# A GELU feed-forward block: the opening loads issued from two engines, b1 from a third, and the warm-up fed from a constant

## The chip, the cores and the metric

The kernel runs on one NeuronCore of a Trainium2 chip. The metric is the device time of one execution in microseconds (us); lower is better. Before the change the median of 3 runs is 96.36 us (96.36 to 96.37).

## The reference

The reference is a two-layer feed-forward block in bfloat16 for 2048 tokens, 448 features and 1792 hidden units:

```python
def reference(x, w1, b1, w2, b2):          # x (1,2048,448), w1 (448,1792), w2 (1792,448)
    h = jnp.einsum("bsd,df->bsf", x, w1) + b1
    h = jax.nn.gelu(h, approximate=True)
    return jnp.einsum("bsf,fd->bsd", h, w2) + b2
```

## The kernel before

**Layers and chunks.** The 2048 tokens are cut into four chunks of 512 columns. Layer 1 ("l1") of a chunk computes 14 tiles of 128 hidden units by 512 tokens. The 448 features are contracted in three full 128-row slices and a remainder of 64 rows; two tiles of neighbouring hidden units run their remainders at the same time on the two halves of TensorE's rows (`half`, line 226), and the full slices run as passes of 512 columns (`full`, line 218). ScalarE applies GELU with the bias `b1_f` to each finished tile (line 326). Layer 2 ("l2", line 303) multiplies the result with w2, and VectorE adds b2 (line 345). TensorE's order is written out by hand: l1 of chunks 0 and 1, l2 of chunk 0, l1 of chunk 2, l2 of chunk 1, and so on. Eight PSUM banks are used in turn.

**The opening.** Layer 1 needs x with features on the partitions. For chunks 1 to 3 the DMA transposes x on the way in (line 154). For chunk 0, x is loaded plainly in two halves into `xn_sb` (lines 162 and 163), TensorE transposes it with sixteen small matmuls against an identity (line 203), and VectorE and ScalarE copy the six results from PSUM to `xT_sb` (lines 339 and 322). b1 is loaded as 14 rows of 128 and turned by one more small matmul (line 194), which stands between the second and the third group of transposes. Before all that TensorE runs eleven passes of 256 columns over a tile of zeros (line 189), whose results are never used.

**The first block of layer 1** (`opening_block`) takes eight tiles of hidden units side by side, one to a PSUM bank: eight passes with the first feature slice (k = 0), eight with the second (k = 1), then the third slices and the remainders: 24 full passes, and 8 halves, which run in pairs. The waits in it are on pieces of w1: k = 0 in two column pieces (`sem_w10[0]` and `sem_w10[1]`, line 136), k = 1, 2 and 3 for the first 1024 hidden units (`sem_w1[k]`, line 140), and, ahead of the next block, the "rest", which is the other 768 hidden units in two transfers (`sem_w1r`, lines 141 and 144). The eighth pass of k = 0 goes to the bank that the turned b1 occupied, so it waits for VectorE's copy of b1 (`sem_b1`).

**The queues.** SP issues, in this order: x's two halves, w1 k = 0 in two pieces, w1 k = 1, 2, 3, the rest of w1 in two transfers, four transposing loads of x's chunk 1, w2 in two parts, b2, the other eight transposing loads, and then the output. ScalarE issues only the b1 load at the start and one output at the end. GpSimd builds the identity and issues nothing.

Of the kernel before, what the change touches and what calls it, by code (L numbers as in the profile page):

```python
# [5 lines left out]
ACT = mybir.ActivationFunctionType  # L6
ALU = mybir.AluOpType
BF16 = mybir.dt.bfloat16
FP32 = mybir.dt.float32


def bass_standalone__dense_activation_gelu__prompt_kernel(
# [8 lines left out]
    B, S, D = x.shape  # L21
    F = w1.shape[1]
    P = 128
# [8 lines left out]
    NFT = F // P  # L32

    KROW = [0, 128, 256, 320]
    NKT = len(KROW)

    WCUT = 8 * P

    W0_PIECES = [(0, 4), (4, 8)]
# [12 lines left out]
    XBANK = 1  # L52
    NB = 8

    NWARM = 11
    WN = 256

    OCUT = 256
# [21 lines left out]
    with ExitStack() as es:  # L80
# [3 lines left out]
        w2_sb = sb("wo_sb", [P, NFT, D], BF16)  # L84
        xn_sb = sb("xn_sb", [P, STC, D], BF16)
        ident = sb("ident", [P, P], BF16)
        zeros = sb("zeros", [P, WN], BF16)
        act_junk = sb("act_junk", [P, 8], BF16)
        b1n_sb = sb("bin_sb", [NFT, P], BF16)
        b1_f = sb("bi_f", [P, NFT], FP32)  # L90
# [8 lines left out]
        sem_w1r = S_("sem_w1r")  # L99
# [2 lines left out]
        sem_xn = [S_(f"sem_xn{i}") for i in range(2)]  # L102
        sem_b1n = S_("sem_b1n")
        sem_x = [None] + [S_(f"sem_x{i}") for i in range(1, NSC)]
        sem_zero = S_("sem_zero")
        sem_id = S_("sem_id")
        sem_xtp = S_("sem_xtp")
        sem_xTd = S_("sem_xTd")
# [21 lines left out]
            src = ps[XBANK + n][:, 0:2 * P * len(parts)]  # L130
            return to, src.rearrange("p (k t) -> p k t", k=len(parts))

        def load_w1(eng):
            with nc.allow_non_contiguous_dma(reason="w1 column pieces"):
                for i, (a, b) in enumerate(W0_PIECES):
                    eng.dma_start(  # L136
                        w1_sb[:, 0, a * P:b * P], w1[0:P, a * P:b * P]
                    ).then_inc(sem_w10[i], 16)
                for k, r in list(enumerate(KROW))[1:]:
                    eng.dma_start(w1_sb[:, k, 0:WCUT], w1[r:r + P, 0:WCUT]).then_inc(sem_w1[k], 16)  # L140
                eng.dma_start(  # L141
                    w1_sb[:, 0:3, WCUT:F], w1[0:3 * P, WCUT:F].rearrange("(k p) f -> p k f", p=P)
                ).then_inc(sem_w1r, 16)
                eng.dma_start(w1_sb[:, 3, WCUT:F], w1[KROW[3]:D, WCUT:F]).then_inc(sem_w1r, 16)

        def load_w2(eng, i):
            a, b = W2_PIECES[i]
# [12 lines left out]
        @block.sync  # L160
        def _(sp):
            sp.dma_start(xn_sb[:, 0:2, :], x0_view[:, 0:2, :]).then_inc(sem_xn[0], 16)  # L162
            sp.dma_start(xn_sb[:, 2:4, :], x0_view[:, 2:4, :]).then_inc(sem_xn[1], 16)  # L163
            load_w1(sp)
            load_xT(sp, 1)
            for i in range(len(W2_PIECES)):
                load_w2(sp, i)
            sp.dma_start(b2_bc[:, :], b2.partition_broadcast(P)).then_inc(sem_b2, 16)
            for c in range(2, NSC):
                load_xT(sp, c)  # L170
            for j in range(NST - 1):
                sp.wait_ge(sem_osb, j + 1)
                sp.dma_start(out_dram(j), out_sb[:, j, :]).then_inc(sem_od, 16)
            sp.wait_ge(sem_od, 16 * NST)

        @block.gpsimd
        def _(pool):
            pool.memset(ident[:, :], 0.0).then_inc(sem_id, 1)  # L178
            pool.wait_ge(sem_id, 1)
            pool.affine_select(  # L180
                out=ident[:, :], in_=ident[:, :], compare_op=ALU.not_equal, fill=1.0,
                base=0, pattern=[[-1, P]], channel_multiplier=1,
            ).then_inc(sem_id, 1)

        @block.tensor
        def _(pe):
            pe.wait_ge(sem_zero, 1)
            for _i in range(NWARM):
                pe.matmul(ps[0][:, 0:WN], lhsT=zeros[:, 0:P], rhs=zeros[:, :], start=True, stop=True)  # L189
            pe.wait_ge(sem_id, 2)  # L190
            for n, (_, parts) in enumerate(XPARTS):
                if n == 2:
                    pe.wait_ge(sem_b1n, 16)
                    pe.matmul(  # L194
                        ps[NB - 1][:, 0:NFT], lhsT=b1n_sb[:, :], rhs=ident[0:NFT, 0:NFT],
                        start=True, stop=True,
                    ).then_inc(sem_b1T, 1)
                for h, k in parts:
                    if (h, k) in ((0, 0), (1, 0)):
                        pe.wait_ge(sem_xn[h], 16)  # L200
                    for t in range(2):
                        col = parts.index((h, k)) * 2 * P + t * P
                        mm = pe.matmul(  # L203
                            ps[XBANK + n][:, col:col + P],
                            lhsT=xn_sb[:, 2 * h + t, KROW[k]:KROW[k] + P],
                            rhs=ident[:, :],
                            start=True, stop=True,
                        )
                mm.then_inc(sem_xtp, 1)
# [7 lines left out]
            def full(c, ft, k, start, stop):  # L217
                return pe.matmul(  # L218
                    bank("g", order.index((c, ft)))[:, :],
                    lhsT=w1_sb[:, k, ft * P:(ft + 1) * P],  # L220
                    rhs=xT_sb[:, k, c * SC:(c + 1) * SC],
                    start=start, stop=stop,
                )
# [11 lines left out]

            def opening_block(first, second):

                fts = first + second
                for n, ft in enumerate(fts):
                    for i, (a, _) in enumerate(W0_PIECES):  # L240
                        if ft == a:
                            pe.wait_ge(sem_w10[i], 16)
                    if n == 0:
                        pe.wait_ge(sem_xTd, 2)
                    elif n == NB - 1:
                        pe.wait_ge(sem_b1, 1)
                    elif XPARTS[n - XBANK][0] == "a":
                        pe.wait_ge(sem_xTa, sum(e == "a" for e, _ in XPARTS[:n - XBANK + 1]))
                    elif n - XBANK >= 4:
                        pe.wait_ge(sem_xTd, sum(e == "d" for e, _ in XPARTS[:n - XBANK + 1]))  # L250
                    full(0, ft, 0, True, False)
                pe.wait_ge(sem_w1[1], 16)
                for n, ft in enumerate(fts):
                    full(0, ft, 1, False, False)
                pe.wait_ge(sem_w1[2], 16)
                pe.wait_ge(sem_w1[3], 16)
                for n, ft in enumerate(first):
                    full(0, ft, SLOTS[n % 2][2], False, False)
                for n, ft in enumerate(first):
                    half(0, ft, *HALVES[n % 2], False, True).then_inc(sem_l1, 1)  # L260
                for n, ft in enumerate(second):
                    half(0, ft, *HALVES[n % 2], False, False)
                for n, ft in enumerate(second):
                    full(0, ft, SLOTS[n % 2][2], False, True).then_inc(sem_l1, 1)
# [48 lines left out]

        @block.scalar
        def _(act):
            act.dma_start(b1n_sb[:, :], b1.rearrange("(c p) -> c p", p=P)).then_inc(sem_b1n, 16)
            act.wait_ge(sem_zero, 1)
            act.activation(act_junk[:, :], zeros[:, 0:8], ACT.Gelu_apprx_tanh)  # L318
            for n, (e, parts) in enumerate(XPARTS):
                if e == "a":  # L320
                    act.wait_ge(sem_xtp, n + 1)
                    act.copy(*x_part(n, parts)).then_inc(sem_xTa, 1)  # L322
            act.wait_ge(sem_b1, 1)
            for i, (c, ft) in enumerate(order):
                act.wait_ge(sem_l1, i + 1)
                act.activation(  # L326
                    g_sb[:, ft, c * SC:(c + 1) * SC], bank("g", i)[:, :], ACT.Gelu_apprx_tanh,
                    bias=b1_f[:, ft:ft + 1], scale=1.0,
                ).then_inc(sem_g, 1)
            act.wait_ge(sem_osb, len(outs))  # L330
            act.dma_start(out_dram(NST - 1), out_sb[:, NST - 1, :]).then_inc(sem_od, 16)

        @block.vector
        def _(dve):
            dve.memset(zeros[:, :], 0.0).then_inc(sem_zero, 1)  # L335
            for n, (e, parts) in enumerate(XPARTS):
                if e == "d":
                    dve.wait_ge(sem_xtp, n + 1)
                    dve.tensor_copy(*x_part(n, parts)).then_inc(sem_xTd, 1)  # L339
            dve.wait_ge(sem_b1T, 1)  # L340
            dve.tensor_copy(b1_f[:, :], ps[NB - 1][:, 0:NFT]).then_inc(sem_b1, 1)  # L341
            dve.wait_ge(sem_b2, 16)
            for n, (j, c0, c1) in enumerate(outs):
                dve.wait_ge(sem_l2, n + 1)
                dve.tensor_tensor(  # L345
                    out=out_sb[:, j, c0:c1], in0=bank("o", n)[:, 0:c1 - c0], in1=b2_bc[:, c0:c1],
                    op=ALU.add,
                ).then_inc(sem_osb, 1)
# [28 lines left out]
```

## Time and profile before

| what | value |
|---|---|
| median of 3 runs | 96.36 us (96.36 to 96.37) |
| the profiled execution, own time | 96.84 us |
| its span, first to last instruction | 95.1 us |
| TensorE (PE) busy | 90.5 us, 95% of the span |
| ScalarE (ACT) busy | 36.1 us, 38% |
| VectorE (DVE) busy | 11.9 us, 13% |
| x halves to `xn_sb`, issue to landing | 2.6 and 2.7 us |
| w1 k = 0 pieces, issue to landing | 3.6 and 3.7 us |
| w1 k = 1 to 3, issue to landing | 4.3 to 5.1 us |
| w1 rest, issue to landing | 7.4 and 7.6 us |

The profiled execution lasted 0.48 us longer than the median of the plain runs, and 1.74 us of its own time lies outside the span. A line of the timeline gives start, length, engine, source line, operation, tiles (written <- read) and count; in brackets stands how long the engine had been idle and what ended the idleness. "SPq" and "ACTq" are an engine's instruction queue, where DMAs are issued; "PEld" is the weight load of a matmul. Matmuls are pipelined, so the length of one is more than the distance from one start to the next.

### The profile page before, as it was taken

The numbers are of one execution on the slowest core, as the hardware profiler recorded it, in microseconds if no ns is written. First come the engines' busy times: TensorE is split into PE (matmuls) and PEld (weight loads), VectorE is DVE, ScalarE is ACT, GpSimd is POOL, SyncE is SP. The second block draws the span as 40 slices with busy tenths as digits, with TensorE's granted clock in tenths as the row PEclk, the third lists the DMA queues.
The fourth block names the chain that finished last, engine by engine and source line by source line (L and its number), as shares of the span: only waits on it lengthen the run. The fifth ranks groups of instructions, "written<-read, shape, count | busy, mean of one in ns | idle before, by whom it ended". The sixth has DMA issues, their size and how long they took to land.

```text
span 95.1 us, 1155 instructions
## 1 busy us (share of the span) xinstructions
PE 90.5 (95%) x484; PEld 43.8 (46%) x490; DVE 11.9 (13%) x22; ACT 36.1 (38%) x61; POOL 0.7 (1%) x6
## 2 busy tenths in 40 slices
PE   5999989999999999999999999999999999999990
PEld 4654243434345555434335555434435555555670
DVE  0240000000000222200000222200000222222130
ACT  3340699959495000049586000039577000000000
POOL 2000000000000000000000000000000000000000
DMA  1899999996520111010000111010000110111111
GB/s 37 257 310 320 101 210 340 358 146 118 108 55 0 48 48 48 22 33 0 0 3 0 48 48 35 13 55 0 0 0 0 48 40 14 43 48 55 48 48 48
DMA packets 12385, 7.50 MB, mean 79 GB/s; under 512 B 7004, under 2 KB 11996, under 8 KB 12380
## 3 DMA queue, kind: packets, MB, share of 16 engines
q1 hardware_dynamic: 12208, 7.31, 32.1%
q10 hardware_dynamic: 172, 0.12, 0.4%
q8 instruction: 4, 0.07, 0.2%
q14 instruction: 1, 0.01, 0.0%
HBM read 4.02 MB, written 1.84 MB: 62 GB/s over the span
## 4 chain that ended last, share of the span: by engine, by line
PE 84%; DMA 8%; SPq 4%; issue 1%; DVE 0%
PE ps L303 45%; PE ps L218 33%; DMA wi_sb<-in_w_dram 8%; PE ps L226 6%; SPq L140 1%; SPq L136 1%; SPq L141 0%; SPq L163 0%; SPq L162 0%; DVE out_sb L345 0%
## 5 line engine op out<-in xcount | busy, mean ns | idle before, releaser
L326 ACT ACTIVATE g_sb<-ps,bi_f 128x512 bf16<-128x512 f32 x56 | 33.3, 700 | 33.8 <-PE ps L226 33.8
L303 PE MATMUL ps<-wo_sb,g_sb 128*128 128x448 bf16 (+2 forms) x238 | 42.9, 341 | 0.0
L218 PE MATMUL ps<-xT_sb,wi_sb 128*128 128x512 bf16 x162 | 37.2, 379 | 1.0 <-issue 0.5
L303 PEld LDWEIGHTS ps<-wo_sb,g_sb 128*128 128x128 bf16 x238 | 23.1, 98 | 19.7
L218 PEld LDWEIGHTS ps<-xT_sb,wi_sb 128*128 128x128 bf16 x168 | 15.6, 98 | 21.8 <-issue 3.6
L345 DVE TENSOR_TENSOR out_sb<-ps,bo_bc 128x448 bf16<-128x448 f32 (+2 forms) x17 | 10.2, 597 | 76.8 <-PE ps L303 76.8
L226 PE MATMUL ps<-xT_sb,wi_sb 64*128 64x512 bf16 x56 | 7.4, 379 | 0.0
L226 PEld LDWEIGHTS ps<-xT_sb,wi_sb 64*128 64x128 bf16 x56 | 2.1, 94 | 4.8 <-issue 3.4
L189 PE MATMUL ps<-zeros 128*128 128x256 bf16 x11 | 2.5, 418 | 1.1 <-DVE zeros L335 1.1
L189 PEld LDWEIGHTS ps<-zeros 128*128 128x128 bf16 x11 | 1.5, 143 | 1.6 <-DVE zeros L335 1.1
L322 ACT CAST xT_sb<-ps 128x256 bf16<-128x256 f32 (+1 forms) x3 | 1.3, 443 | 1.8 <-PE ps L203 1.8
L339 DVE CAST xT_sb<-ps 128x256 bf16<-128x256 f32 (+1 forms) x3 | 1.5, 514 | 3.4 <-PE ps L203 3.4
L203 PE MATMUL ps<-ident,xn_sb 128*128 128x128 bf16 x16 | 1.8, 287 | 0.0
L318 ACT ACT_TABLE_LOAD x1 | 1.3, 1283 | 1.4 <-PEq L362 1.4
L203 PEld LDWEIGHTS ps<-ident,xn_sb 128*128 128x128 bf16 x16 | 1.4, 132 | 0.4 <-issue 0.4
L180 POOL TENSOR_SCALAR_AFFINE_SELECT ident<-ident 128x128 bf16<-128x128 bf16 x1 | 0.3, 294 | 0.2 <-POOL ident L178 0.2
L335 DVE MEMSET zeros<- 128x128 uint32 x1 | 0.2, 165 | 0.8 <-PEq L362 0.8
L318 ACT ACTIVATE act_junk<-zeros 128x8 bf16<-128x8 bf16 x1 | 0.2, 208 | 0.0
L178 POOL MEMSET ident<- 128x128 bf16 x1 | 0.2, 205 | 0.3 <-POOLq L362 0.3
L194 PE MATMUL ps<-ident,bin_sb 14*128 14x14 bf16 x1 | 0.2, 188 | 0.0
L194 PEld LDWEIGHTS ps<-ident,bin_sb 14*128 14x128 bf16 x1 | 0.1, 97 | 0.2 <-issue 0.2
L341 DVE COPY bi_f<-ps 128x14 f32<-128x14 f32 x1 | 0.2, 163 | 0.0
(4 smaller groups left out, 0.4 us busy)
## 6 DMA issues: line engine op xcount, KB each, us to landing
out_dram<-out_sb SPq DMA_DIRECT2D x15, 112.0 KB, 1.7
wo_sb<-in_w_dram SPq DMA_DIRECT2D x2, 784.0 KB, 6.6
wi_sb<-in_w_dram SPq DMA_DIRECT2D x3, 256.0 KB, 4.7
wi_sb<-in_w_dram SPq DMA_DIRECT2D x1, 576.0 KB, 7.4
xn_sb<-in_x_dram SPq DMA_DIRECT2D x2, 224.0 KB, 2.7
wi_sb<-in_w_dram SPq DMA_DIRECT2D x2, 128.0 KB, 3.7
wi_sb<-in_w_dram SPq DMA_DIRECT2D x1, 192.0 KB, 7.6
xT_sb<-in_x_dram SPq DMA_TRANSPOSE x12, 4.0
```

The lines of the kernel that those rows point to most:

```text
L136: eng.dma_start(w1_sb[:, 0, a * P:b * P], w1[0:P, a * P:b * P]).then_inc(sem_w10[i], 16)
L140: eng.dma_start(w1_sb[:, k, 0:WCUT], w1[r:r + P, 0:WCUT]).then_inc(sem_w1[k], 16)
L189: pe.matmul(ps[0][:, 0:WN], lhsT=zeros[:, 0:P], rhs=zeros[:, :], start=True, stop=True)
L203: mm = pe.matmul(ps[XBANK + n][:, col:col + P], lhsT=xn_sb[:, 2 * h + t, KROW[k]:KROW[k] + P], rhs=ident[:, :], start=True, stop=True,)
L218: return pe.matmul(bank("g", order.index((c, ft)))[:, :], lhsT=w1_sb[:, k, ft * P:(ft + 1) * P], rhs=xT_sb[:, k, c * SC:(c + 1) * SC], sta ...
L226: return pe.matmul(bank("g", order.index((c, ft)))[:, :], lhsT=w1_sb[lo:lo + HALF, k, ft * P:(ft + 1) * P], rhs=xT_sb[lo:lo + HALF, k, c * ...
L303: mm = pe.matmul(bank("o", n)[:, 0:c1 - c0], lhsT=g_sb[:, ft, j * P:(j + 1) * P], rhs=w2_sb[:, ft, c0:c1], start=(ft == 0), stop=(ft == NF ...
L318: act.activation(act_junk[:, :], zeros[:, 0:8], ACT.Gelu_apprx_tanh)
L322: act.copy(*x_part(n, parts)).then_inc(sem_xTa, 1)
L326: act.activation(g_sb[:, ft, c * SC:(c + 1) * SC], bank("g", i)[:, :], ACT.Gelu_apprx_tanh, bias=b1_f[:, ft:ft + 1], scale=1.0,).then_inc( ...
L339: dve.tensor_copy(*x_part(n, parts)).then_inc(sem_xTd, 1)
L345: dve.tensor_tensor(out=out_sb[:, j, c0:c1], in0=bank("o", n)[:, 0:c1 - c0], in1=b2_bc[:, c0:c1], op=ALU.add,).then_inc(sem_osb, 1)
```

## The change

The change touches only the first microseconds of the program.

- x's second half, w1's second k = 0 piece and w1's k = 2 slice are issued by ScalarE; SP keeps x's first half, the first k = 0 piece, k = 1, k = 3 and the rest.
- b1 is loaded by GpSimd, after it has built the identity.
- The matmul that turns b1 moves from the transposes into the opening block, behind seven of the eight k = 0 passes. The eighth k = 0 pass moves to just ahead of the eighth k = 1 pass.
- The tile of zeros, its memset on VectorE and `sem_zero` are gone. The warm-up passes read the built-in constant 1.0 and wait for nothing of VectorE, and there are 13 of them instead of 11. ScalarE's first activation reads a built-in 0.0.

```diff
-    NWARM = 11
+    NWARM = 13
...
-        def load_w1(eng):
+        def load_w1(eng, which):
...
         def _(sp):
             sp.dma_start(xn_sb[:, 0:2, :], x0_view[:, 0:2, :]).then_inc(sem_xn[0], 16)
-            sp.dma_start(xn_sb[:, 2:4, :], x0_view[:, 2:4, :]).then_inc(sem_xn[1], 16)
-            load_w1(sp)
+            load_w1(sp, [("0", 0), 1, 3, "rest"])
             load_xT(sp, 1)
...
             ).then_inc(sem_id, 1)
+            pool.dma_start(b1n_sb[:, :], b1.rearrange("(c p) -> c p", p=P)).then_inc(sem_b1n, 16)
 
         @block.tensor
         def _(pe):
-            pe.wait_ge(sem_zero, 1)
+            ones_w = nc.const_aps.tensor(1.0, [P, P], BF16)
+            ones_x = nc.const_aps.tensor(1.0, [P, WN], BF16)
             for _i in range(NWARM):
-                pe.matmul(ps[0][:, 0:WN], lhsT=zeros[:, 0:P], rhs=zeros[:, :], start=True, stop=True)
+                pe.matmul(ps[0][:, 0:WN], lhsT=ones_w, rhs=ones_x, start=True, stop=True)
             pe.wait_ge(sem_id, 2)
             for n, (_, parts) in enumerate(XPARTS):
-                if n == 2:
-                    pe.wait_ge(sem_b1n, 16)
-                    pe.matmul(
-                        ps[NB - 1][:, 0:NFT], lhsT=b1n_sb[:, :], rhs=ident[0:NFT, 0:NFT],
-                        start=True, stop=True,
-                    ).then_inc(sem_b1T, 1)
...
                 fts = first + second
-                for n, ft in enumerate(fts):
+                for n, ft in enumerate(fts[:-1]):
...
-                    elif n == NB - 1:
-                        pe.wait_ge(sem_b1, 1)
...
                     full(0, ft, 0, True, False)
+                pe.wait_ge(sem_b1n, 16)
+                pe.matmul(
+                    ps[NB - 1][:, 0:NFT], lhsT=b1n_sb[:, :], rhs=ident[0:NFT, 0:NFT],
+                    start=True, stop=True,
+                ).then_inc(sem_b1T, 1)
                 pe.wait_ge(sem_w1[1], 16)
                 for n, ft in enumerate(fts):
+                    if n == NB - 1:
+                        pe.wait_ge(sem_b1, 1)
+                        full(0, ft, 0, True, False)
                     full(0, ft, 1, False, False)
...
         def _(act):
-            act.dma_start(b1n_sb[:, :], b1.rearrange("(c p) -> c p", p=P)).then_inc(sem_b1n, 16)
-            act.wait_ge(sem_zero, 1)
-            act.activation(act_junk[:, :], zeros[:, 0:8], ACT.Gelu_apprx_tanh)
+            act.dma_start(xn_sb[:, 2:4, :], x0_view[:, 2:4, :]).then_inc(sem_xn[1], 16)
+            load_w1(act, [("0", 1), 2])
+            zero = nc.const_aps.tensor(0.0, [P, 8], FP32)
+            act.activation(act_junk[:, :], zero, ACT.Gelu_apprx_tanh)
...
-            dve.memset(zeros[:, :], 0.0).then_inc(sem_zero, 1)
```

`load_w1` takes a list of the parts to issue on the given engine: `("0", i)` is piece i of k = 0, a number is that k, and `"rest"` stands for the two last transfers. The transfers themselves have the same shapes as before.

## The prediction

> **What bounds the kernel now.** The summary says that PE is busy for 95% of the span, so I read the chain that ended last, in order of time, to find where it leaves PE.
>
> ```profile
> 4.02 0.43 SPq L141
> 4.45 0.04 issue
> 4.50 7.63 DMA wi_sb<-in_w_dram
> 12.12 0.05 issue
> 12.17 2.76 PE ps L218 x12
> ```
>
> From 12.17 to the end the chain is PE, without a gap above 0.16 us. Before 12.17 it is SP's row of issues and the landing of the last w1 rest at 12.12. So the change, all of it ahead of 12.17, is worth what it moves the start of the second block, and nothing else. What PE itself did up to there is in the timeline of the opening.
>
> ```profile
> 0.83 0.17 DVE L335 MEMSET zeros<- 128x128 uint32 x1 [0.83 <-PEq L362]
> ...
> 1.05 2.53 PE L189 MATMUL ps<-zeros 128*128 128x256 bf16 x11 [1.05 <-DVE zeros L335]
> ...
> 3.50 0.58 PE L203 MATMUL ps<-ident,xn_sb 128*128 128x128 bf16 x4
> ...
> 4.02 0.19 PE L194 MATMUL ps<-ident,bin_sb 14*128 14x14 bf16 x1
> ...
> 4.14 1.25 PE L203 MATMUL ps<-ident,xn_sb 128*128 128x128 bf16 x12
> ...
> 5.45 3.14 PEld L218 LDWEIGHTS ps<-xT_sb,wi_sb 128*128 128x128 bf16 x16 [0.23 <-DMA wi_sb<-in_w_dram]
> ```
>
> The transposes begin as x's first half lands (issue 0.74 plus 2.6). The opening block begins at 5.45, 0.23 us after PE could have, on w1's first k = 0 piece (issue 1.66 plus 3.6 or 3.7). In a narrow window its last full pass starts at 11.50, and passes start 0.216 us apart, so the opening block is done at 11.72 and PE loses 0.45 us to the rest of w1. There are thus two DMA gates, 0.23 and 0.45 us, around a PE chain. Then I asked in half microseconds how well the DMA engines were fed.
>
> ```profile
> 2.00:2.50 0.50, 0.50 (x4) 0.33 (x3) 0.00 (x0) 0.50 (x1) 0.00 (x0) 1.00 0.63 182
> ...
> 3.00:3.50 0.50, 0.50 (x3) 0.13 (x2) 0.00 (x0) 0.00 (x0) 0.00 (x0) 1.00 0.97 354
> 3.50:4.00 0.50, 0.50 (x5) 0.32 (x4) 0.09 (x1) 0.00 (x0) 0.00 (x0) 1.00 0.91 196
> 4.00:4.50 0.50, 0.50 (x6) 0.46 (x6) 0.34 (x1) 0.37 (x1) 0.00 (x0) 1.00 0.51 139
> 4.50:5.00 0.50, 0.50 (x8) 0.50 (x6) 0.42 (x1) 0.21 (x1) 0.00 (x0) 1.00 0.70 199
> ```
>
> The last two columns are the DMA engines' busy share and GB/s. They move 354 at 3.0, but 139 to 199 from 3.5 to 5.0, just when w1's 128 KB pieces are due, of which SP issues one every 0.46 us. After 5.0 the share is 0.9 and over.
>
> **The change part by part**, on the profiled execution's clock.
>
> Warm-up: PE need not wait for VectorE's memset. GpSimd and SP begin their own work at 0.73 and 0.74, so PE starts at 0.75, 0.30 us earlier. Eleven passes started 0.211 us apart (1.05 to 3.16), so thirteen end at 0.75 + 13 x 0.211 = 3.50, against 3.37 before.
>
> x: the halves are issued at 0.74 side by side instead of at 0.74 and 1.20, and share the engines. The first half can't land before 3.35; it hardly lands after 3.9, when both had landed before. I take 3.55, nearer to the early end, since the share of 0.63 at 2.0 leaves room for a second feeder. The transposes then start at 3.65 instead of 3.50.
>
> Transposes: b1's matmul leaves. Four transposes from 3.50 would have let the fifth start at 3.88; it started at 4.14, so 0.26 us goes, and the second half, then landed, puts no wait in its place. Early transposes start 0.107 us apart, the last ones 0.055 (5.12 and 5.17 in narrow windows): PE's real pace doubles at about 5.0, 3.95 us after its first warm-up pass, though the clock column says 1.00 all along. With PE starting 0.30 us earlier, the pace rises between 4.7 and 5.0; I take 4.9. Twelve transposes from 3.65 at 0.107 reach 4.93, four at 0.055 reach 5.15. PE was through them at 5.23 before, so PE itself gains only 0.08 us here.
>
> The Trainium skill ("TensorE: Matmul & The Clock Gate", section "Part 1: The HAM clock gate (the "warmup" mystery)") says that the clock rises after a busy window of about 3.4 us which runs freely and doesn't start with the kernel. By that rule the earlier start buys no fixed 0.30 us, and the rise may stay at 5.0: 0.05 us or so of my sum.
>
> w1's first k = 0 piece: issued at 1.20 instead of 1.66. With the same 3.7 us it lands at 4.9; with ScalarE's 128 KB piece moving beside it at 325 GB/s (the row of 6 to 9 us), 0.4 later, 5.3. The opening block starts at 5.2, range 5.05 to 5.4, instead of 5.45.
>
> Opening block: it took 6.27 us (5.45 to 11.72). b1's matmul now stands in it, 0.12 us by the distance 4.02 to 4.14. The passes are the same ones. It ends at 5.2 + 6.39 = 11.59. The new wait of PE for b1 has 17 full passes and all halves queued behind it. GpSimd's load isn't in the trace: it is issued at about 1.5 (the identity's last step runs from 1.17 to 1.46) and is needed at 5.2 + 7 x 0.216 = 6.7. The landing times in the trace run from 1.7 to 7.6 us; at 2.7, the row nearest in time and load, b1 is there at 4.2, at the far end at 9.1. I take nothing. The second wait, for VectorE's copy (0.16 us), has seven passes of cover, 1.5 us.
>
> w1's rest: issued 1.45 us earlier (SP has three issues fewer ahead of it). If the landing kept its 7.6 us it would come at 10.7; if bytes alone decide, it stays at 12.1. The idle shares from 1.5 to 5.0 add up to 0.96 us of all engines; half of it won back gives 11.65. I take that.
>
> The Trainium skill ("DMA: Bandwidth & Descriptors", section "Issuing engines are not separate DMA queues") speaks against the change: DMAs of all issuers run on the same 16 engines, and a second issuer saves only issuing time, which is usually small. The row of 4.00 to 4.50, share 0.51, shows engines that were waiting for something; by the rule alone the gate would stay near 12.1.
>
> The rest: ScalarE's three issues cost 0.41 to 0.65 us each (rows of SP's L163 and of its own L316), so its table load (1.28) and first activation (0.21) end at 3.6 to 4.3 instead of 2.9; its first copy, at 4.12 before, moves to at most 4.35 and is needed by the third pass, at 5.6. Without that cover of 0.9 us PE would wait the difference. SP's transposing loads, w2 and b2 move up by at most 1.45 us; w2 is needed at 28.1, so nothing is gained, and the transposing loads still queue behind the rest of w1.
>
> Sum: the second block starts at 11.70 (the gate at 11.65, then the same 0.05), 0.47 us earlier. The profiled execution goes from 96.84 to 96.37, and the median by the same amount, from 96.36 to 95.89. The median was 0.48 below the profiled time, and I can't tell whether the 0.45 us gate is part of that; it stays in the range.
>
> **The rivals.**
>
> No change, a transfer or a PE chain that doesn't move: either the rest of w1 lands at 12.1 again, because the slowest engine's bytes decide (for it: 0.9 and over busy from 5 to 9 us), or plain runs have no DMA gate and PE's own chain decides, where 0.08 gained and 0.12 lost cancel. It gives 96.2 to 96.5. Against it: two gates would have to vanish together, or the starved stretch be of no use. Chance 0.20.
>
> Slower, PE's pace: both halves of x land only at 3.9, PE is idle from 3.50 to 4.0, and the rise of its pace is counted anew, 3.95 us from 4.0, to 7.95. The sixteen slow transposes last to 5.71. An opening pass at the slow pace costs 0.422 (twice 0.211), so 5.3 of 28 slots are done by 7.95, and the other 22.7 x 0.216, 0.22 of gaps and 0.12 for b1 bring the block's end to 13.19, the second block to 13.24: 1.07 later, 97.4. It decides from the point where the rise comes after about 6.1, since each us of delay costs half a us and the block has 12.12 - 11.59 = 0.53 to spare. For it: sharing x is sure, and the warm-up ends 0.15 ahead of my start of the transposes. Against it: a gap of half a us is short beside 2.8 us of work before it. Chance 0.15; b1 landing after 9.1 (98.2) or the like, 0.05.
>
> **How the numbers follow.** Faster has 0.60: 0.47 gained, own range 95.45 (opening from 5.05, rest in time, pace up at 4.7) to 96.15 (the first gate alone gains). A measurement of this kernel can tell about 0.2%, or 0.19 us, from no change. The range goes from 95.45 through no change to 96.9, a rise of the pace at about 7.1; it leaves out the worse half of the slower cases and a little below, under 0.2 together.
>
> **What would show it.** Right: warm-up passes from 0.75; x's halves landing within 0.2 us of each other at 3.4 to 3.7; no b1 matmul among the transposes; opening passes from about 5.2; DMA shares above 0.8 from 3.5 to 5.0; the second block from about 11.7. Wrong: the rest of w1 still ending PE's idleness at 12.1; opening passes starting over 0.4 us apart; PE idle in front of the b1 matmul.

## The result, and the profile after

The change made the kernel slower: a median of 97.31 us over 22 executions against 96.50 us for the kernel before over 22 beside it, a ratio of 1.006 (95% interval 1.0041 to 1.0079). On two other occasions the changed kernel, unedited or as good as unedited, came to 1.0034 (1.0013 to 1.0055) and 1.0042 (1.0017 to 1.0067). The three executions of the kernel before that were shown first, 96.36 to 96.37, lay near the low end of its 96.22 to 97.20. A few executions of most kernels here are some 2 us longer than the rest; the ratios leave these out, the medians hold them.

The profiled execution after the change lasted 97.52 us, its span 95.7. The chain that ended last (start, length, what):

```profile
1.66 6.42 DMA wi_sb<-in_w_dram
8.08 0.05 issue
8.13 2.98 PE ps L221 x13
11.11 0.97 PE ps L229 x8
12.08 3.56 PE ps L221 x16
```

The transfer in the chain is no longer the rest of w1, but k = 1, issued at 1.66 and landed at 8.08. Before, k = 1 had landed at 6.93 and nobody waited for it. From 8.13 on PE runs through; the second block has lost its gate. The timeline of the opening shows the rest:

```profile
0.79 2.93 PE L198 MATMUL ps<-const-bfloat16-1.0 128*128 128x256 bf16 x13 [0.79 <-PEq L372]
...
4.09 1.69 PE L206 MATMUL ps<-ident,xn_sb 128*128 128x128 bf16 x16 [0.37 <-DMA xn_sb<-in_x_dram]
...
5.61 1.67 PE L221 MATMUL ps<-xT_sb,wi_sb 128*128 128x512 bf16 x7
...
7.22 0.09 PEld L255 LDWEIGHTS ps<-ident,bin_sb 14*128 14x128 bf16 x1 [0.42 <-DMA bin_sb<-in_b_dram]
...
8.13 2.98 PE L221 MATMUL ps<-xT_sb,wi_sb 128*128 128x512 bf16 x13 [0.73 <-DMA wi_sb<-in_w_dram]
```

In the kernel before, the first twenty opening passes had run through without a gap:

```profile
5.45 4.49 PE L218 MATMUL ps<-xT_sb,wi_sb 128*128 128x512 bf16 x20
```

After the change, PE starts to warm up 0.26 us earlier and then waits for x; the transposes start at 4.09, not 3.50; the opening passes at 5.61, not 5.45; the b1 matmul follows them at 7.22, just after b1's landing at 7.17; and in front of the k = 1 passes PE stands idle for 0.8 us. The opening block ends at 12.89. Before, the second block had started at 12.17, so it starts 0.72 us later; the first pass of layer 2 shows nearly the same difference, 28.63 against 27.93. The page's list of DMA issues (issuer, KB each, median us to landing) has the reason, two lines from before and four from after:

```profile
wi_sb<-in_w_dram SPq DMA_DIRECT2D x3, 256.0 KB, 4.7
xn_sb<-in_x_dram SPq DMA_DIRECT2D x2, 224.0 KB, 2.7
...
wi_sb<-in_w_dram SPq DMA_DIRECT2D x2, 256.0 KB, 6.5
wi_sb<-in_w_dram ACTq DMA_DIRECT2D x1, 256.0 KB, 6.6
xn_sb<-in_x_dram SPq DMA_DIRECT2D x1, 224.0 KB, 3.2
xn_sb<-in_x_dram ACTq DMA_DIRECT2D x1, 224.0 KB, 3.4
```

A 256 KB slice took a median of 4.7 us to land before and 6.5 or 6.6 now, half of x 2.7 and now 3.2 or 3.4. What was issued side by side landed side by side: x's halves at 3.95 and 4.13 (3.37 and 3.90 before), k = 1 and k = 2 at 8.08 and 8.31 (6.93 and 7.77 before). And in half microseconds, the last columns being the DMA engines' share and GB/s:

```profile
4.00:4.50 0.50, 0.41 (x5) 0.44 (x6) 0.00 (x1) 0.00 (x0) 0.00 (x0) 1.00 0.94 195
4.50:5.00 0.50, 0.50 (x8) 0.50 (x6) 0.50 (x2) 0.29 (x1) 0.00 (x0) 1.00 0.98 201
```

The stretch that I had read as starved engines is still slow, 195 and 201 GB/s, with the engines now busy 0.94 and 0.98 of the time. The second issuer filled the idle shares, and no more bytes moved for it.

### The profile page after: what moved, and what is told of

Same layout as the page of the kernel before. It is cut to its first block, busy times and chain, and to the rows that moved or that the text cites. A ratio compares the mean times of both kernels' runs of the same rounds, so it can differ in the third digit from the quotient of the medians.

```text
span 95.7 us, 1164 instructions
## 1 busy us (share of the span) xinstructions
PE 91.3 (95%) x492; PEld 44.2 (46%) x492; DVE 11.9 (12%) x21; ACT 35.9 (38%) x61; POOL 1.3 (1%) x7
## 4 chain that ended last, share of the span: by engine, by line
PE 89%; DMA 7%; SPq 1%; DVE 0%; issue 0%
PE ps L313 44%; PE ps L221 37%; PE ps L229 7%; DMA wi_sb<-in_w_dram 7%; SPq L145 0%; SPq L170 0%; DVE out_sb L355 0%
## 5 line engine op out<-in xcount | busy, mean ns | idle before, releaser
L221 PE MATMUL ps<-xT_sb,wi_sb 128*128 128x512 bf16 x168 | 38.3, 380 | 0.7 <-DMA wi_sb<-in_w_dram 0.7
L198 PE MATMUL ps<-const-bfloat16-1.0 128*128 128x256 bf16 x13 | 2.9, 414 | 0.8 <-PEq L372 0.8
L198 PEld LDWEIGHTS ps<-const-bfloat16-1.0 128*128 128x128 bf16 x13 | 1.8, 141 | 1.5 <-issue 0.8
L191 POOL DMA_DIRECT2D bin_sb<-in_b_dram x1 | 0.6, 647 | 0.2 <-issue 0.2
```

Source lines behind the costliest of these rows:

```text
L191: pool.dma_start(b1n_sb[:, :], b1.rearrange("(c p) -> c p", p=P)).then_inc(sem_b1n, 16)
L198: pe.matmul(ps[0][:, 0:WN], lhsT=ones_w, rhs=ones_x, start=True, stop=True)
L221: return pe.matmul(bank("g", order.index((c, ft)))[:, :], lhsT=w1_sb[:, k, ft * P:(ft + 1) * P], rhs=xT_sb[:, k, c * SC:(c + 1) * SC], sta ...
```

## The experiments

Three theories were to be told apart. O, order: two issuers' transfers share the DMA engines, so what is needed first lands together with what is needed later. G: GpSimd's load of b1 is the cost. C: the warm-up, or idleness in it, moves the rise of PE's pace. All ratios are to the kernel before, run beside the experiment; the diffs are abridged to the calls that move.

**k = 2 back on SP.**

```diff
-load_w1(sp, [("0", 0), 1, 3, "rest"]);  load_w1(act, [("0", 1), 2])
+load_w1(sp, [("0", 0), 1, 2, 3, "rest"]);  load_w1(act, [("0", 1)])
```

> The changed kernel with one edit: w1's k = 2 slice goes back to SP, behind k = 1. Theory O (two issuers share the DMA engines, so what is needed first lands together with what is needed later): k = 1 no longer shares with k = 2, lands at 6.9 to 7.4 instead of 8.08, PE's idle stretch in front of the k = 1 passes falls from 0.8 us to 0.2 or less, and the time goes back to the kernel before within 0.2% (ratio 0.998 to 1.002). Theory G (GpSimd's load of b1 is what holds, by landing at 7.17 and by disturbing the others): b1 still lands at about 7.2 and the ratio stays at 1.004 to 1.008. Theory C (the earlier and longer warm-up moves the rise of PE's pace): nothing changes, 1.006.

Measured: 0.9998 (0.9973 to 1.0023). With this one edit no loss is left that could be told. PE's timeline:

```profile
4.23 1.09 PE L206 MATMUL ps<-ident,xn_sb 128*128 128x128 bf16 x16 [0.51 <-DMA xn_sb<-in_x_dram]
5.48 1.67 PE L221 MATMUL ps<-xT_sb,wi_sb 128*128 128x512 bf16 x7 [0.16 <-DVE xT_sb L349]
7.09 0.18 PE L255 MATMUL ps<-ident,bin_sb 14*128 14x14 bf16 x1
7.20 2.76 PE L221 MATMUL ps<-xT_sb,wi_sb 128*128 128x512 bf16 x12
```

k = 1 landed at 5.73, earlier than expected, b1 at 5.91, and the passes run through. x's first half is as late as in the changed kernel (4.10), so that lateness alone doesn't make the loss. What the two issuers' queues moved from 4 to 6 us (packets, MB, share of the 16 engines' time; q1 is SP's queue, q10 ScalarE's) shows the difference, first in the changed kernel, then here:

```profile
q1 hardware_dynamic: 133, 0.24, 57.8%
q10 hardware_dynamic: 130, 0.20, 30.4%
...
q1 hardware_dynamic: 332, 0.61, 91.0%
q10 hardware_dynamic: 64, 0.05, 7.3%
```

In the changed kernel k = 2 on ScalarE's queue takes nearly half of the bytes, while k = 1 waits for its own on SP's. All the bytes of the two were fewer as well, 0.44 MB against 0.66, but that isn't due to the second queue as such: the kernel before moved 0.47 MB in the same stretch from one queue.

**x's second half back on SP.**

```diff
+sp.dma_start(xn_sb[:, 2:4, :], ...)    # behind the first half
-act.dma_start(xn_sb[:, 2:4, :], ...)
```

> The changed kernel with one edit: x's second half goes back to SP, behind the first half; ScalarE keeps the second k = 0 piece and k = 2. Theory O: the first half lands at 3.4 to 3.7 instead of 3.95 and the transposes start that much earlier, but k = 1 still shares with k = 2 and stays the gate at about 8, so the time moves by less than 0.2 us (ratio 1.003 to 1.007). Theory G: the same time, 1.006. Theory C: opening passes at the fast pace from 5.3, time down by 0.3 us.

Measured: 1.0134 (1.0066 to 1.0201), median 98.80, but two of the six executions took 97.00 and 97.33 and four 98.66 to 99.07, so the ratio is the size of neither group. All three theories missed. The profile is of the quickest execution. In it ScalarE's loads start with the k = 0 piece and k = 2, ahead of x's second half, which landed at 4.94; PE stood idle between the two halves' transposes:

```profile
3.99 0.38 PE L207 MATMUL ps<-ident,xn_sb 128*128 128x128 bf16 x4 [0.27 <-DMA xn_sb<-in_x_dram]
4.98 0.84 PE L207 MATMUL ps<-ident,xn_sb 128*128 128x128 bf16 x12 [0.61 <-DMA xn_sb<-in_x_dram]
```

That is O in another place: k = 2, which is needed last, landed at 5.16, ahead of k = 1 (6.63) and 0.2 us behind the half of x that PE was waiting for. What held the four executions near 99 no profile shows.

**b1 on ScalarE, behind its loads.**

```diff
-pool.dma_start(b1n_sb, ...)
+act.dma_start(b1n_sb, ...)             # behind load_w1(act, ...)
```

> The changed kernel with one edit: b1 is loaded by ScalarE behind its three other loads, not by GpSimd. Theory G: without GpSimd's load k = 1 lands at about 7 and the ratio to the kernel before falls to 1.000 or below. Theory O: b1 lands earlier than 7.17, but k = 1 still at about 8, which was the later of the two; ratio unchanged, 1.004 to 1.008. Theory C: unchanged too.

Measured: 1.0084 (1.0053 to 1.0115). Without GpSimd's load k = 1 still lands late, at 7.50, k = 2 at 7.69, and b1 itself at 7.87, later than O had it; PE was idle for 0.96 us in front of the b1 matmul, which also hides the wait for k = 1. The late k = 1 doesn't come from GpSimd's load, so G falls.

**All of x and w1 back on SP.**

```diff
+SP: x first half, x second half, ("0", 0), ("0", 1), 1, 2, 3, "rest";  ScalarE: nothing
```

> The changed kernel with all x and w1 loads back on SP in the order of the kernel before; GpSimd's b1 load, the constant warm-up of 13 passes and the place of the b1 matmul stay. Theory O: x's first half lands at 3.4, k = 1 at 6.9, no gap in front of the k = 1 passes unless b1 makes one; ratio to the kernel before 0.996 to 1.002. Theory G: b1 at 7 or later still stops PE behind seven passes, 0.3 us or more, ratio 1.003 to 1.008. Theory C: 1.004 or more, with the rise of the pace later than 5.0.

Measured: 1.0026 (1.0002 to 1.0049). x's first half is back at 3.38, k = 1 at 6.67, b1 at 5.00, no gap. In the profiled execution the seven first opening passes took 2.21 us instead of 1.67: PE's pace rose only at about 6.5. The ratio lies between O's stretch and the two others': the landings are as O has them, the late rise in this one profile is as C has it, and b1 made no wait, against G.

**The warm-up alone**, put into the kernel before.

```diff
-NWARM = 11; tile of zeros, sem_zero
+NWARM = 13; built-in 1.0
```

> The kernel before with the warm-up of the change alone: 13 passes over the built-in 1.0, no tile of zeros. Every load, the b1 matmul and its place are those of before. If the warm-up is harmless (theory O): first pass at 0.78 instead of 1.05, transposes from 3.5 as before, ratio 0.998 to 1.002. Theory C (the warm-up costs): 1.002 or more, about what putting all loads back on SP still lost (1.0026).

Measured: 0.9991 (0.9968 to 1.0014). No harm of the warm-up shows.

**All on SP, and b1 on ScalarE as before.**

```diff
-pool.dma_start(b1n_sb, ...)            # in the version with all of x and w1 on SP
+act.dma_start(b1n_sb, ...)             # first on ScalarE
```

> All loads of x and w1 on SP in the old order and b1 on ScalarE as before; what is left of the change is the warm-up and the b1 matmul behind seven passes. If GpSimd's load of b1 costs anything beside the order of the loads (theory G), this is 0.2% or more faster than the run with all loads on SP and b1 on GpSimd (1.0026), so 1.000 or below; if not, 1.001 to 1.004.

Measured: 1.0018 (0.9994 to 1.0042). Against 1.0026 with GpSimd that is no difference that could be told. Against the run before this one it differs only in the place of the b1 matmul. In its timeline the passes on both sides of that matmul start 0.43 us apart (6.91 and 7.34), where passes follow each other at 0.216, so the matmul takes 0.21 us out of the opening block; among the transposes it stood in time that PE partly spent waiting for w1. The two intervals overlap, so this price is seen in the profile alone.

**k = 3 on ScalarE instead of k = 2.**

```diff
-load_w1(sp, [("0", 0), 1, 3, "rest"]);  load_w1(act, [("0", 1), 2])
+load_w1(sp, [("0", 0), 1, 2, "rest"]);  load_w1(act, [("0", 1), 3])
```

> The changed kernel with k = 2 and k = 3 exchanged: SP issues x's first half, the first k = 0 piece, k = 1, k = 2, rest; ScalarE x's second half, the second k = 0 piece, k = 3. Theory O (any 256 KB slice in flight beside k = 1 delays it): k = 1 lands at 7.0 or later, PE idles in front of it, ratio 1.004 to 1.008. Theory P (it is the pair k = 1 and k = 2, which read neighbouring rows of w1 at the same time): k = 1 lands below 6.5 as with k = 2 on SP, ratio 0.998 to 1.002.

Measured: 1.0034 (1.0006 to 1.0061). k = 1 landed at 7.48, k = 3 at 7.67, and PE waited:

```profile
6.99 0.18 PE L255 MATMUL ps<-ident,bin_sb 14*128 14x14 bf16 x1
7.53 2.76 PE L221 MATMUL ps<-xT_sb,wi_sb 128*128 128x512 bf16 x12 [0.37 <-DMA wi_sb<-in_w_dram]
```

So k = 3 from ScalarE's queue delays k = 1 as k = 2 does; it isn't the pair k = 1 and k = 2. From 4 to 6 us the two queues moved 0.29 MB each.

**k = 2 on SP and 15 warm-up passes.**

```diff
-NWARM = 13                             # in the version with k = 2 on SP
+NWARM = 15
```

> k = 2 back on SP as in the first of these runs, and 15 warm-up passes instead of 13, so that PE works from 0.78 to about 3.95, when x's first half lands, instead of idling for 0.5 us. If that idle stretch delays the rise of PE's pace in some executions (theory C), the median falls by 0.1 to 0.4 us, ratio 0.995 to 0.999; if not, 0.998 to 1.002 as with 13.

Measured: 0.9989 (0.9961 to 1.0016). No difference from 13 passes could be told.

**The changed kernel again**, unedited.

> The changed kernel once more, unedited, beside the next kernels on their chip, for a second profile. Theory O: k = 1 and k = 2 land within 0.4 us of each other at 7.4 to 8.3, PE idles 0.3 to 1.0 us between the k = 0 and the k = 1 passes, ratio 1.004 to 1.008. If the late k = 1 of the first profile was an accident of one execution, k = 1 lands below 6.8 here and no such gap is seen.

Measured: 1.0034 (1.0013 to 1.0055). k = 1 landed at 7.58, k = 2 at 7.76, as O says, but no gap came of it:

```profile
5.80 2.00 PE L221 MATMUL ps<-xT_sb,wi_sb 128*128 128x512 bf16 x7
7.74 0.18 PE L255 MATMUL ps<-ident,bin_sb 14*128 14x14 bf16 x1
7.84 2.76 PE L221 MATMUL ps<-xT_sb,wi_sb 128*128 128x512 bf16 x12
```

In this execution the transposes ran at the slow pace throughout, the passes began at 5.80 and the first seven took 2.00 us, so PE came to k = 1 at 7.84, after its landing. The late k = 1 is in every profile of this arrangement; what it costs depends on how far PE has come, and here the time went into the late x and the slow passes.

**Filling the idle stretch between the halves.**

```diff
+if n == 2: six more warm-up passes     # in the version with x's second half on SP
```

> The run with x's second half on SP (median 98.80, half its executions near 99.0) with six more warm-up passes of 256 columns on TensorE between the transposes of x's first half and those of the second, where PE had idled for 0.8 us. Theory C (an idle stretch in the opening delays the rise of PE's pace in many executions): the executions near 99 go, median 96.7 to 97.4, though six passes of work are added. If the idle stretch itself or the landing of x's second half is the cost, the median stays above 98.

Measured: 1.0124 (1.0103 to 1.0144), median 97.95. In its four executions, 97.82 to 98.00, none lay near 99, as C has it, but the median missed the expected stretch: the six passes ran from 4.74 to 5.90, past the landing of x at 5.25. With four executions this stays inconclusive.

**Two versions meant to beat both**: ScalarE issues b1 first, whose matmul stands ahead of the transposes.

```diff
+NWARM = 14, built-in 1.0; if n == 0: b1 matmul
+ScalarE: b1, x second half, ("0", 1);  SP: x first half, ("0", 0), 1, 2, 3, "rest"       # first version
+ScalarE: b1, ("0", 1);  SP: x first half, x second half, ("0", 0), 1, 2, 3, "rest"       # second version
```

> A version meant to beat both: constant warm-up of 14 passes; ScalarE issues b1 first, then x's second half and the second k = 0 piece; SP x's first half, the first k = 0 piece, k = 1, 2, 3, rest in this order; the b1 matmul stands ahead of the transposes, where PE waits for x anyway. Theory O: k = 1 lands below 7 and makes no gap, b1's 0.12 us leave the opening block, second block at 11.3 to 11.6, ratio 0.994 to 0.998. If sharing x's landing costs as much as the earlier pieces bring, 0.998 to 1.002.

> The same with x's second half on SP behind the first, so that ScalarE issues b1 and the second k = 0 piece alone. x's first half lands at 3.4 to 3.6, the second at 4.0 to 4.4 (the piece beside it), so PE may idle between the transposes of the two halves. Theory O: 0.996 to 1.000, not better than the version with the second half on ScalarE. If idle stretches delay the rise of the pace (theory C), 1.002 or more.

Measured: 1.0035 (1.0010 to 1.0060) for the first, 0.9985 (0.9963 to 1.0006) for the second. The intervals don't meet, though the versions differ only in who issues x's second half. In the first it was issued at 1.42, behind b1 and behind SP's k = 0 piece, and landed at 4.62; in the second at 1.18, landing at 4.03. The piece that overtook it landed at 4.05 and was needed at 5.9. In the profile of the first, PE's pace also rose late, at 6.4 (4.9 in the second's), and what part of the difference that makes isn't known. I had expected the order the other way round. The second has the lowest ratio of all the versions, but 1 lies within its interval: nothing here is shown to beat the kernel before.

**k = 2 later on ScalarE.**

```diff
+load_w1(act, [("0", 1)]);  table load, first activation;  load_w1(act, [2])
```

> The changed kernel with ScalarE's load of k = 2 moved behind its table load and first activation, from 1.68 to about 3.2. If being in flight together is the cost (theory O): k = 1, issued at 1.66, is 1.5 us ahead, lands at 6.9 or earlier, with k = 2 and k = 3 landing after it, and the ratio falls to 0.998 to 1.002. If the issuer is the cost (two queues as such): k = 1 still at 7.4 or later, ratio 1.004 to 1.008.

Measured: 1.0042 (1.0017 to 1.0067), but not what was meant. Two lines of the timeline:

```profile
1.67 1.28 ACT L329 ACT_TABLE_LOAD   x1 [1.67 <-PEq L373]
1.74 0.38 ACTq L150 DMA_DIRECT2D wi_sb<-in_w_dram  x1
```

The load of k = 2 stands behind the table load in the program and was issued during it, at 1.74 instead of 1.68. The run is thus a third measurement of the change: k = 1 landed at 7.69, and PE's gap was 0.45 us. Some 0.35 of it was a wait for b1, which landed at 7.47, the rest for k = 1.

**k = 2 alone on ScalarE, in the kernel before.**

```diff
+SP: ..., 1, 3, "rest";  ScalarE: b1, table load, first activation, k = 2
```

> The kernel before with one part of the change alone: w1's k = 2 is issued by ScalarE behind its table load and first activation, at about 2.95, while SP issues k = 1 at 2.60 and k = 3 at 3.07. Theory O: k = 2 now shares with k = 1, which lands at 7.2 to 8 instead of 6.93, within 0.4 us of k = 2; the k = 1 passes, due at 7.2 there, are held by up to 0.6 us, ratio 1.001 to 1.006. If sharing is harmless in the order of before: k = 1 at 6.7 to 7.0, ratio 0.998 to 1.001.

Measured: 1.0041 (1.0019 to 1.0064). For the same reason k = 2 was issued at 1.50, ahead of both k = 0 pieces and of k = 1. In the profile it landed at 4.96 and k = 1 at 6.66, so the two didn't meet and neither expectation is tested; x's second half came at 4.25 instead of 3.90. The profiled execution was the quickest of its twelve, 96.31, and doesn't show the loss, so the path of the loss stays open. That this part alone, at this place, loses about as much as the whole change is measured.

**The kernel before without warm-up.**

```diff
-NWARM = 11
+NWARM = 0
```

> The kernel before without its eleven warm-up passes, all else equal. PE then starts with the transposes at 3.5, and if its pace rises only some 3 to 6 us after it has begun to work, the opening passes run at 0.42 us for 1 to 4 us more than before: 0.5 to 2 us longer, ratio 1.005 to 1.02. If the pace did not depend on earlier work, the ratio would be 1.000.

Measured: 1.0124 (1.0086 to 1.0161). The transposes start as before, at 3.49, and the passes then run slowly for long:

```profile
5.70 5.84 PE L218 MATMUL ps<-xT_sb,wi_sb 128*128 128x512 bf16 x20
```

Twenty passes take 5.84 us, against 4.49 in the kernel before. The starts are 0.427 us apart up to 8.2. The rise comes between the starts at 8.23 and 8.57, and the price of the late pace is 1.2%.

**k = 2 waits for x's first half.**

```diff
+load_w1(act, [("0", 1)]);  act.wait_ge(sem_xn[0], 16);  load_w1(act, [2])
```

> The changed kernel with ScalarE's load of k = 2 issued only once x's first half has landed, at about 4.0 instead of 1.68; it stays on ScalarE. If being in flight together is the cost (theory O): k = 1, 2.3 us ahead, lands below 6.9, b1 too, the passes of k = 0 and k = 1 run without a gap over 0.2 us; k = 2 must land by 9.0 to be in time, and if it does the ratio is 0.997 to 1.002. If a second issuer as such is the cost: k = 1 at 7.4 or later, ratio 1.003 to 1.008.

Measured: 1.0268 (1.0200 to 1.0335). Half of O's expectation held: k = 1 landed at 5.94 and b1 at 5.56, with k = 2 still on ScalarE. So it isn't the second issuer as such that delays k = 1, but its slice in flight at the same time. Nor is it SP's transposing loads, which move up with the change: their first was issued at 3.62 here and at 3.63 in the changed kernel, against 5.03 before. And the total rate can't be the whole reason: from 4 to 6 us both queues together moved 0.60 MB here and 0.59 with k = 3 on ScalarE, but SP's 0.54 here and 0.29 there, where k = 1 landed at 7.48. The other half failed:

```profile
3.86 0.34 ACTq L150 DMA_DIRECT2D wi_sb<-in_w_dram  x1
...
11.47 1.04 PE L221 MATMUL ps<-xT_sb,wi_sb 128*128 128x512 bf16 x4 [1.75 <-DMA wi_sb<-in_w_dram]
```

k = 2, issued at 3.86, landed at 11.43, after the rest of w1 (9.65), with the four transposing loads of SP in flight as well. PE stood idle for 1.75 us.

## Why the prediction was wrong

The forecast was 95.89 us, a gain of 0.47; the loss was 0.6%, and the time lies outside the range. One thing held throughout: the change is worth what it moves the second block. In all 18 profiles the execution's own time is 68.88 to 68.95 us more than the start of layer 2's first pass (96.84 and 27.93 before, 97.52 and 28.63 after). By the prediction's own steps:

**Warm-up.** Right: from 0.79 to 3.51, for 0.75 to 3.50.

**x.** Mis-sized. I took 3.55 and called 3.9 the far end; it landed at 3.95, and in the other profiles with the halves side by side at 3.84 to 4.10. I had counted on a faster ramp; from 2.0 to 2.5 the engines moved 219 GB/s for 182, while ScalarE's half, landing 0.18 us behind, took its share of them. The opening passes began at 5.61, not at 5.2.

**Pace.** I let the rise follow PE's first pass by 3.95 us. In the changed kernel it came at 5.45, and at about 6.5 in its second profile. Over the profiles with PE starting at 0.8 it came anywhere from 4.0 or earlier (x on SP) to about 6.5 (all on SP), with nothing in the opening to explain it. That agrees with the Trainium skill ("TensorE: Matmul & The Clock Gate", section "Part 1: The HAM clock gate (the "warmup" mystery)"), by which the deciding window runs freely. A single profile thus carries a chance of half a microsecond or more either way. The clock column can't show the rise: the trace's records of the clock begin only with it (at 5.5 and 6.5 us in the two profiles of the change), and before the first record the column reads 1.00.

**k = 0 piece.** Better than taken: at 4.57, for 4.9 to 5.3. That gate went as forecast, and its gain was lost because x was late.

**b1.** I priced it from the nearest row, 2.7 us after issue, though that row was of loads issued before the crowd. It landed at 7.17, 5.5 us after its issue. PE lost nothing to that: the b1 matmul starts 0.31 us behind the pass before it, as with k = 2 back on SP, where b1 had landed at 5.91. In the third measurement of the change the wait for b1 did cost 0.35. With all of x and w1 on SP the same load landed after 3.3 us, on ScalarE behind three other loads after 5.7, so what it met on the way counted more than who issued it. The matmul itself was mis-sized: it takes 0.21 us out of the opening block, for 0.12; its going from the transposes had rightly been read as 0.26.

**k = 1: the step that failed.** I wrote of the opening block that "the passes are the same ones" and let it run through, 6.39 us. k = 1 has no line in the sum. Of the slices moved I costed those that had been gates before, the first k = 0 piece and the rest, and not those that would become gates. The rows were there: the idleness for w1 lay at 5.45 and 12.12, and k = 1, at 6.93 against its first use at 7.2, had 0.25 us to spare. Giving nearly half of the bytes to k = 2, which is needed 1.7 us later, ate more than that: k = 1 landed at 8.08. The steps add up: 0.41 us for the opening passes (5.61, for 5.2), 0.09 for the b1 matmul and 0.80 for the wait on k = 1, on top of the forecast end of the block at 11.59, give 12.89, as measured. In the second profile of the change the opening passes were 0.60 late (5.80), slow passes took 0.33 and k = 1 nothing; with b1's 0.09 that gives 12.61, and the second block started at 12.60. So the term that was missing is the largest in one profile and stayed hidden behind x and the pace in the other.

**The rest of w1.** Better than taken: 10.84, for 11.65 and 12.12 before. It won 1.3 us that PE couldn't use. The starved stretch, my reason for it, was misread: the shares rose and the bytes didn't. And the rest landed at 10.76 in a profile with all loads on SP as well (the warm-up alone), so the 12.12 of the first profile was in part that execution's own. The median shows the same: by the fixed 68.9 us, its 96.36 puts the second block 0.48 us earlier than in the profile, at about 11.7, which is when PE itself was ready (11.72). This is an estimate, but by it the gate of 0.45 us wasn't in those three runs at all, and most of the 0.47 of the forecast couldn't have been won there; PE's own chain, 11.59 for 11.72, would have given 0.13.

**The rule against the change.** The Trainium skill ("DMA: Bandwidth & Descriptors", section "Issuing engines are not separate DMA queues") says that DMAs of all issuers interleave on the same engines. I weighed it as "no gain". The queues' rows (0.24 and 0.20 MB from 4 to 6 us) agree with the page, and the runs add that the interleaving of a load needed first with one needed later is itself a loss.

**The rivals.** None named it. The slow-pace rival had the right first step (x late, PE idle for 0.6 us) and the wrong sequel; idleness and slow passes did contribute in the second profile of the change.

**Slips in the sums.** The idle shares from 1.5 to 5.0 add up to 0.93 us, not 0.96, which leaves the gate at 11.65. The low end of the range, 95.45, doesn't follow from its terms: 5.05 + 6.39 is 11.44, 0.73 before 12.17, which gives 95.63. Neither bears on the outcome.

How much of the 0.34 to 0.60% is k = 2 beside k = 1 is known only roughly: taking it back gives 0.9998 and, with 15 warm-up passes, 0.9989, so all of it within the 0.25% of those intervals, which overlap that of the weakest measurement of the change (1.0013 to 1.0055) by up to 0.1%. Of the profiles with x's halves side by side, the five with a 256 KB slice on ScalarE beside k = 1 have k = 1 at 7.5 to 8.1, and SP's queue moved 0.24 to 0.31 MB from 4 to 6 us; the three without have it at 5.7 to 7.1, with 0.51 to 0.61 MB. Sharing with one more slice would account for some 0.9 us (k = 2 came 0.87 after k = 1 in the version with k = 2 on SP).

The rest is in the tail of the landing. The trace shows a slice land in sixteen parts, each of which adds one to the semaphore, and PE waits for the last. Of k = 1's parts the eighth came at 6.18 and the last at 8.08 in the changed kernel; with k = 2 on SP these were 5.22 and 5.73. Half of the slice was thus late by about what sharing accounts for, and the last parts by much more. Such a tail also came without a slice beside it: with 15 warm-up passes fifteen parts were there at 6.35 and the last at 7.07, and in the run with the filled idle stretch fifteen at 6.58 and the last at 8.51. What makes the tail, and why the engines' total rate between 4 and 6 us differs from profile to profile, stays open.

## What to carry to other kernels

One issuing queue was also an order of arrival: with all loads of x and w1 on SP they landed in the order of their issue (before, from 3.37 to 12.12). Before a load moves to a second issuer, list for every transfer in flight when it lands and when it is first used, those without a wait today first of all: the spare time of the nearest one is what the change may take. A small first gain at a gate is worth nothing if the next slice in line had less to spare.

## What the runs showed of the hardware

- A DMA on ScalarE is issued without waiting for a table load ahead of it in the program (1.74 and 1.50 us, with the table load running from 1.67 and 1.43). A wait on a semaphore does delay it (3.86).
- PE's pace doubled anywhere from 4.0 (or a little earlier) to 6.5 us into the span with a warm-up that began at 0.8, while the profile's clock column, which has no record before the rise, read 1.00 throughout; without warm-up between 8.2 and 8.6, for 1.2% of the time.
- With a 256 KB slice from each of two queues in flight, the two queues moved 0.24 and 0.20 MB from 4 to 6 us, and the slices landed 0.2 us apart, at 8.08 and 8.31; with both slices on one queue it moved 0.61 MB, and the first landed at 5.73.
- The last of a slice's sixteen parts can land long after the others: of k = 1 fifteen had landed at 6.58 and the last came at 8.51, in the run with the filled idle stretch.
- 256 KB issued from the second queue at 3.86, with k = 1, k = 3, the rest of w1 and four transposing loads of the first still to land, took 7.6 us to land.
- In the profiles of the kernel before and of the changed one the loads fell to 139 to 256 GB/s for 1.5 to 2 us between 3.5 and 6.0, with the engines up to 0.98 busy; with k = 2 on SP they kept 271 to 389 in one profile and 235 to 343 in another. What slows them isn't settled.
